# A long convolution that feeds an eight-expert layer: the third group's first input transforms moved into the first sort, its later loads asked for earlier, the filter spectrum loaded once and copied

## The chip, the core and the metric

One Trainium2 chip, one NeuronCore of it. TensorE (PE) multiplies; VectorE (DVE), ScalarE (ACT) and GpSimd (POOL) do the element-wise work, POOL also issues the gathers and scatters by row; SyncE (SP) does nothing but issue transfers, in the order in which they were written. The metric is the time of one execution in device microseconds (us).

## What is computed

Eight sequences of 5696 tokens with 128 features each are convolved along time with one filter per feature (through FFTs of twice the length), and every token of the result goes through one of eight experts, the one with the highest gate logit:

```python
L = 2 * S
Xf = np.fft.rfft(x, n=L, axis=1)
Hf = np.fft.rfft(h, n=L, axis=0)
y = np.fft.irfft(Xf * Hf[None], n=L, axis=1)[:, :S, :]
x = y.reshape(B * S, D)
logits = x @ w_gate
expert_idx = np.argmax(logits, axis=1)
for e in range(E):
    mask = expert_idx == e
    out[mask] = gate_w[mask, None] * (np.maximum(x[mask] @ w1[e], 0.0) @ w2[e])
```

## The kernel before

The batch is cut into three **groups** of 2, 3 and 3 sequences (SPLIT). Each goes through three phases, and the experts run beside the later ones.

- **Phase A** (`steps_a`, `phase_a`): the first FFT step. A loaded piece `xt` of `x` is split by ACT and DVE (or POOL) into two parts, `xc`; PE makes `pa` from it (three matmuls for the real and three for the imaginary half); a copy puts it into `ut`, and SP stores `ut` to the DRAM tensor `U`. A group of 3 has 36 such pieces: 12 rounds (`ig`) of 3 sequences. Group 0 does this alone, group 1 among the first sort, group 2 as a "guest" of the second sort (class `Guest`).
- **Phase B** (`phase_b`): the 48-point step, 120 frequencies `q`, four to a unit (`qb`). Per unit SP loads `uq` from `U`, the matrices `mt` and `mi`, and the filter's spectrum `hh` from `HS`, twice, into the upper and the lower half of the partitions. Per frequency (a **bin**): PE makes `xp` from `uq` and `mt`; DVE multiplies by the spectrum (three instructions, `zt`, `xs`, `xs`: the product); DVE or POOL adds (`combine`; DVE for the first ALONE bins); PE makes `vp` from `zt` and `mi`; ACT copies it to `vt`, which SP stores to `V`. The four steps follow each other at 1, 2, 4 and 5 bins' distance. In group 2 three of four matrices come in split form, `mt<-mqs`, and that load is issued on POOL's queue (line 456), from the third unit on.
- **Phase C**, the sort (`phase_c`): the last FFT step `yp`, its transpose `tp`, gate logits and counts `gb`, a chain of small DVE instructions that gives every token a row, and one scatter of 120 rows by POOL for each slot (`SR<-rt,pi`, line 665), with a POOL `memset` behind each but the last unit's (line 896, size REST). That memset's value is not used. It writes into a tile that the sort doesn't need: `mibufs[3]` in group 0's sort, `hhbufs[2]` in the later ones. A sort of 3 sequences has 24 units of 2 steps and 144 scatters.
- **Tables** (`tables`): some 25 small DVE instructions make from the counts the table `tab`, which says for each tile of 256 rows where its rows start and which expert it has.
- **Experts** (`experts`): per tile SP loads the rows `xr` and, where the expert changes, the weights `wb<-WD`; PE transposes (`mx`), multiplies by both layers (`mh`, `ma`), ACT and DVE take the relu (`hs`).

Every engine works through its instructions in the order in which the program wrote them; `run` writes them, by stream (experts, and `rest`, which holds the other phases), in the order of costs that are summed by hand. `rest` lets a group's tables advance by two pieces with every bin of the next phase B, and lets the experts have a group's tiles (`begin`) when the bins' summed cost is over HEAD.

All xp, vp, pa, and part of the sort's banks share four PSUM banks (tag "cx"); `mh` has two of its own.

Of the kernel before, what the change touches and what calls it, by code (L numbers as in the profile page):

```python
# [23 lines left out]
NB = 48  # L24
# [3 lines left out]
HP = 64  # L28
# [23 lines left out]
ALONE = (0, 14, 10)  # L52
HEAD = (0, 5500, 9000)
# [13 lines left out]
TABLED = 4  # L67
RATE = (0.372, 0.55, 0.28, 0.8, 1.05, 0.6)
# [3 lines left out]
def conv_moe(ctx: ExitStack, tc: tile.TileContext, I, out, B, S, D, E, F, split):  # L72
# [86 lines left out]
    state = {"rests": False, "space": False, "spare": None, "pe": 0.0, "sent": 0.0, "tail": 0}  # L159

# [13 lines left out]
    fcs = load_const("fcs", [MP, 2, QN])  # L174
# [16 lines left out]
    gcs = load_const("gcs", [QN, 2, MP])  # L191
# [7 lines left out]
    jrow = load_const("jrow", [1, total])  # L199
# [66 lines left out]
    def steps_a(gr, tag, bufs):  # L266
        g, nb = gr.g, gr.nb
        srcs = [(I["x"][gr.b0 + b], b) for b in range(nb)]
        tw = 4 * D
        items = []  # L270
        for ig in range(NB // 4):
            for src, b in srcs:
                items.append((ig, src, b))
# [4 lines left out]
        def cut(n):  # L278
            if not split or n >= len(items):
                return  # L280
# [6 lines left out]
        def load(n):  # L287
            if n >= len(items):
                return
            ig, src, b = items[n]  # L290
# [18 lines left out]
        def store(m):  # L309
            n, c = divmod(m, 2)  # L310
            ig, src, b = items[n]
            if b == 0:
                uts[c] = sb.tile([QN, 4, gr.cols], F32, tag=tag, name=f"ut{g}_{ig}_{c}", bufs=bufs)
# [11 lines left out]
        def begin(m):  # L325
            if m == 0:
                cut(0)
            if m % 2 == 0:
                load(m // 2 + fore)
                cut(m // 2 + 1)  # L330
            transform(m)

        return start, begin, store, flush, 2 * len(items)

    def phase_a(gr):
        start, begin, store, flush, M = steps_a(gr, "six", SIX - gr.g)
        half = AT if gr.g == 0 else 750 * RATE[3 * gr.g - 3]
        start()
        for m in range(M + 2):
# [4 lines left out]
            yield half  # L344
# [6 lines left out]
    class Guest:  # L351
        def __init__(self, gr):
            self.start, self.step, self.store, self.flush, self.M = steps_a(gr, "mt", MT)
# [87 lines left out]
    def phase_b(gr):  # L441
# [26 lines left out]
        def load(qb):  # L468
# [8 lines left out]
            if g != 0:  # L477
                hhs[qb] = hhbufs[qb % 3]
                for k in range(2):
# [5 lines left out]
        state, banks, late = {}, {}, []  # L485

# [81 lines left out]
        def inverse(n):  # L568
# [4 lines left out]
            vp = ps.tile([P, 512], F32, tag="cx", name=f"vp{g}_{q}_{c}", bufs=4)  # L573
# [141 lines left out]
    def phase_c(pt, guest=None):  # L715
# [156 lines left out]
        def rank(n):  # L872
# [576 lines left out]
```

## Time and profile before

| | |
|---|---|
| median of 3 runs | 2156.97 us (2149.7 to 2160.83) |
| the profiled execution | 2157.51 us, span 2155.7 us |
| PE busy | 2082.7 us, 97% of the span |
| DVE / ACT / POOL busy | 72% / 52% / 63% |
| DMA engines | share .85 to 1.0 in the first third, .5 to .8 in the second, about .35 in the last |
| granted clock of TensorE | 0.976 on average |

The span falls into stretches that can be told by the tiles in the timeline: phase A of group 0 to 100 us, phase B to 227, the first sort with phase A of group 1 to 391, phase B of group 1 with the experts from 425 on to 690, the second sort with the guest to 932, phase B of group 2 to 1345, the third sort to 1600, experts alone to the end. PE is busy in nearly all of it. It stands still or runs at the lower of its two clock levels (1.2 instead of 2.4 GHz) mainly where one stretch hands over to the next: about 380 to 430, 900 to 985 and 1605 to 1625 us. A row of the timeline has the start, the duration, the engine, the line, what is written and read, how many instructions were merged, and in brackets how long the engine had been idle before and what ended that. A row of the windows view has for each engine the busy time (and instructions) in a stretch, then the granted clock, the share of the DMA engines and GB/s.

### The profile page before, as it was taken

How to read it: one execution, taken by the hardware profiler on the slowest of the kernel's cores; microseconds unless marked ns; L12 is line 12 of the kernel's file. 1: busy time of each engine (PE TensorE's matmuls, PEld its weight loads, DVE VectorE, ACT ScalarE, POOL GpSimd, SP SyncE). 2: the span in 40 equal slices, each digit the busy share in tenths (PEclk: the TensorE clock that was granted, in tenths of full speed). 3: DMA queues.
4: the chain of work that ended last, by engine and by line, in shares of the span. 5: the costliest groups of instructions: out<-in, count | busy, mean ns of one | idle time of the engine just before them, and what ended most of it. 6: DMA issues, size and time to landing. Idle time of an engine off the chain costs nothing.

```text
span 2155.7 us, 47101 instructions
## 1 busy us (share of the span) xinstructions
PE 2082.7 (97%) x14452; PEld 1863.3 (86%) x14452; DVE 1542.5 (72%) x3373; ACT 1114.9 (52%) x2317; POOL 1350.0 (63%) x1569
## 2 busy tenths in 40 slices
PE   9999999799999999989999999999999999999998
PEld 7799777377777889878888888999999999999998
DVE  4698677799997777688888887666665555555554
ACT  5677555143334666534555555555544454444544
POOL 6566388545554388888998775288883444443333
PEclk9999999599999999999999999999999999999999
DMA  8899799999997898868878885656533244343331
GB/s 269 263 289 293 227 297 281 256 237 256 248 267 196 232 276 255 245 168 229 204 205 222 216 203 153 159 132 159 141 103 98 87 132 135 129 133 126 123 121 34
DMA packets 216993, 420.33 MB, mean 195 GB/s; under 512 B 32501, under 2 KB 136235, under 8 KB 216740
## 3 DMA queue, kind: packets, MB, share of 16 engines
q1 hardware_dynamic: 187263, 360.52, 59.7%
q0 software_dynamic: 27072, 55.35, 8.9%
q8 instruction: 117, 1.92, 0.4%
q10 hardware_dynamic: 2405, 1.43, 0.2%
q14 instruction: 136, 1.11, 0.2%
HBM read 582.45 MB, written 154.27 MB: 342 GB/s over the span
## 4 chain that ended last, share of the span: by engine, by line
PE 82%; DMA 9%; DVE 3%; POOL 2%; issue 2%; ACT 1%; SPq 1%; ACTq 0%; POOLq 0%; DVEq 0%
PE mh L167 23%; PE ma L167 22%; PE vp L167 9%; PE xp L167 9%; PE yp L167 5%; PE mx L189 4%; PE pa L167 3%; DMA xt<-x 3%; PE gb L167 2%; DMA wb<-WD 2%; DMA mt<-mq 2%; PE tp L189 1%; PE hp L167 1%; PE lb L189 1%; DMA U<-ut 1%
## 5 line engine op out<-in xcount | busy, mean ns | idle before, releaser
L1173 DVE SCALAR_TENSOR_TENSOR hs<-mh,hs 128x512 fp32r<-128x512 f32 x728 | 501.6, 689 | 387.5 <-ACT hs L1171 381.2
L167 PE MATMUL mh<-xtb,wb 128*128 128x256 f32 x4368 | 706.4, 297 | 23.0 <-DVE hs L1173 5.2
L1171 ACT ACTIVATE hs<-mh 128x512 fp32r<-128x512 f32 x728 | 435.4, 598 | 488.1 <-PE mh L167 475.4
L167 PEld LDWEIGHTS mh<-xtb,wb 128*128 128x128 f32 x4368 | 589.8, 191 | 92.6 <-issue 37.9
L167 PE MATMUL ma<-hs,wb 128*128 128x256 f32 x4368 | 658.3, 287 | 1.7 <-DMA wb<-WD 1.7
L167 PEld LDWEIGHTS ma<-hs,wb 128*128 128x128 f32 x4368 | 574.4, 191 | 2.9 <-DMA wb<-WD 2.7
L665 POOL DMA_INDIRECT SR<-rt,pi x384 | 406.0, 1057 | 196.2 <-issue 58.9
L683 POOL DMA_INDIRECT out<-xr x310 | 305.4, 985 | 354.2 <-ACT hs L1171 172.6
L566 POOL TENSOR_TENSOR zt<-zt,xs 128x384 f32<-128x384 f32 (+1 forms) x276 | 295.8, 1074 | 155.2 <-DVE xs L556 103.9
L603 ACT COPY vt<-vp 96x384 f32<-96x384 f32 x240 | 114.2, 476 | 260.8 <-PE vp L167 256.6
L560 DVE TENSOR_TENSOR xs<-xp,hh 64x384 f32<-64x384 f32 (+1 forms) x360 | 214.8, 597 | 7.8
L167 PE MATMUL vp<-zt,mi 128*96 128x384 f32 x480 | 200.5, 500 | 0.0
L551 DVE TENSOR_TENSOR zt<-xp,hh 128x384 f32<-128x384 f32 (+1 forms) x300 | 173.6, 579 | 28.7 <-PE xp L167 18.4
L167 PE MATMUL xp<-uq,mt 96*128 96x384 f32 (+1 forms) x496 | 177.7, 462 | 8.5 <-DMA uq<-U 5.1
L167 PE MATMUL pa<-xc,fcr 120*120 120x512 f32 x576 | 159.4, 411 | 1.9 <-POOL xc L284 1.0
L556 DVE SCALAR_TENSOR_TENSOR xs<-xp,hh 64x384 f32<-64x384 f32 x240 | 134.3, 560 | 4.2
L167 PE MATMUL yp<-vr,gcr 120*120 120x384 f32 x576 | 119.5, 343 | 7.1 <-ACT ut L317 7.1
L167 PEld LDWEIGHTS vp<-zt,mi 128*96 128x96 f32 x480 | 79.7, 167 | 49.8 <-issue 26.7
L167 PEld LDWEIGHTS pa<-xc,fcr 120*120 120x120 f32 x576 | 99.9, 186 | 25.2 <-DVE rk L884 2.6
L167 PEld LDWEIGHTS xp<-uq,mt 96*128 96x128 f32 x496 | 87.6, 200 | 33.5 <-issue 12.8
L317 DVE COPY ut<-pa 120x512 f32<-120x512 f32 x96 | 65.7, 684 | 68.6 <-PE pa L167 54.7
L749 DVE TENSOR_TENSOR vr<-vq,vr 120x768 fp32r<-120x768 f32 x96 | 91.5, 954 | 31.8 <-ACT vr L748 31.0
(165 smaller groups left out, 2720.9 us busy)
## 6 DMA issues: line engine op xcount, KB each, us to landing
wb<-WD SPq DMA_DIRECT2D x728, 512.0 KB
U<-ut SPq DMA_DIRECT2D x48, 720.0 KB
uq<-U SPq DMA_DIRECT2D x60, 576.0 KB
V<-vt SPq DMA_DIRECT2D x60, 576.0 KB
vq<-V SPq DMA_DIRECT2D x48, 720.0 KB
xt<-x SPq DMA_DIRECT2D x96, 240.0 KB
hh<-HS SPq DMA_DIRECT2D x120, 192.0 KB
xr<-SR SPq DMA_DIRECT2D x155, 130.0 KB
```

The lines of the kernel that those rows point to most:

```text
L167: nc.tensor.matmul(to, lhs, rhs, **kw)
L189: nc.tensor.transpose(dst, src, ident[:n, :n])
L551: nc.vector.tensor_tensor(out=zt, in0=x3, in1=hv[:, 0].broadcast_to([P, PK, cb, D]), op=ALU.mult)
L556: nc.vector.scalar_tensor_tensor(out=xs[to, 0], in0=x3[at, 0], scalar=-1.0, in1=him[:, 0], op0=ALU.mult, op1=ALU.mult)
L560: nc.vector.tensor_tensor(out=xs[to], in0=x3[at], in1=him, op=ALU.mult)
L566: eng.tensor_tensor(out=zt, in0=zt, in1=xs, op=ALU.add)
L603: done = nc.scalar.copy(outs_[qb][:, k0 : k0 + PK, c * cw : (c + 1) * cw], banks.pop(n)[:K2, :iw].rearrange("p (q x) -> p q x", q=PK),)
L665: s = nc.gpsimd.indirect_dma_start(out=SR[:, :], out_offset=IndirectOffsetOnAxis(ap=pi[:, b : b + 1], axis=0), in_=rt[:, b, :], in_offset= ...
L683: sc = nc.gpsimd.indirect_dma_start(out=out[:, :], out_offset=IndirectOffsetOnAxis(ap=xr[:, s, D + 1 : D + 2].bitcast(I32), axis=0), in_=x ...
L749: nc.vector.tensor_tensor(out=vr[:, 1], in0=src, in1=vr[:, 0].bitcast(F32), op=ALU.subtract)
L1171: done = nc.scalar.activation(hs[:, 0], hp, AF.Relu)
L1173: done = nc.vector.scalar_tensor_tensor(out=hs[:, 1], in0=hp, scalar=0.0, in1=hs[:, 0].bitcast(F32), op0=ALU.max, op1=ALU.subtract)
```

## The change

Seven edits:

1. `phase_a` of group 1 goes on with the first round of group 2: three pieces, six transforms, their six copies all on ACT, two stores to `U`. The guest of the second sort starts from the second round.
2. `phase_b` of group 2 is entered when the second sort writes its last unit's second step, and then asks for the first two units' inputs; its bins follow after the sort, as before.
3. From the third unit on `hh` is loaded once, and ACT copies it to the other partitions in two halves.
4. POOL's filler memset writes into the FFT constants that are no longer needed (`spent`).
5. ALONE of group 1 from 14 to 5: `combine` of bins 5 to 13 from DVE to POOL. HEAD of group 1 from 5500 to 7000: the experts may start two bins later.
6. `vp` of group 1 takes its PSUM bank from `mh`'s two as long as no expert has started.
7. `tables` has one expert per partition, sums over experts by small matmuls (`ah`, `rj`), and has 13 pieces where it had 11.

```diff
-ALONE = (0, 14, 10)
-HEAD = (0, 5500, 9000)
+ALONE = (0, 5, 10)
+HEAD = (0, 7000, 9000)
+AFORE = 1
+SLOW = 2.0
...
+    spent = const.tile([MP, 4, QN], F32, name="spent")
+    fcs, gcs = spent[:, :2], spent[:, 2:]
...
+        items = work(gr)[AFORE * nb :] if after else work(gr)
+        if g == 1:
+            items += work(groups[2])[: AFORE * groups[2].nb]
+        own = len(work(gr))
...
-            cp = nc.scalar.copy if c == 0 else nc.vector.tensor_copy
+            cp = nc.scalar.copy if c == 0 or n >= own else nc.vector.tensor_copy
             cp(uts[c][:, :, b * D : (b + 1) * D], srcv)
             if b == nb - 1:
-                late.append((gr.U[:, lo : lo + 4, :], uts[c]))
+                late.append((to.U[:, lo : lo + 4, :], uts[c]))
...
-            yield half
+            yield half * (SLOW if m >= own else 1)
...
-                for k in range(2):
+                for k in range(2 if qb < 2 else 1):
                     nc.sync.dma_start(hhs[qb][k * HP : k * HP + NB, :QB], HS[:, q : q + QB])
...
+        def double(qb, at):
+            if g and 2 <= qb < QN // QB:
+                hh = hhs[qb][:, at : at + QB // 2]
+                nc.scalar.copy(hh[HP : HP + NB], hh[:NB])
...
-            vp = ps.tile([P, 512], F32, tag="cx", name=f"vp{g}_{q}_{c}", bufs=4)
+            tag, bufs = ("mh", 2) if g == 1 and not live else ("cx", 4)
+            vp = ps.tile([P, 512], F32, tag=tag, name=f"vp{g}_{q}_{c}", bufs=bufs)
...
+        if ask:
+            yield 0
...
+                if k0 == 0:
+                    double(qb, QB // 2)
+                if k0 == QB - 1:
+                    double(qb + 1, 0)
...
-                    idle = hhbufs[2].rearrange("p a b d -> p (a b d)") if g else mibufs[3].rearrange("p a x -> p (a x)")
-                    nc.gpsimd.memset(idle[:, : REST[g]], 0.0)
+                    nc.gpsimd.memset(spent.rearrange("p c q -> p (c q)")[:, : REST[g]], 0.0)
...
+                if guest and (n, k) == (nu - 1, 1):
+                    assert guest.m == guest.M
+                    guest.bins = phase_b(guest.gr, True)
+                    next(guest.bins)
...
-        for k in range(E):
-            if k % 4 == 0:
-                yield
-            e = E - 1 - k if down else k
-            a, b = (e + 1, e) if down else (e, e + 1)
-            nc.vector.tensor_tensor(out=end[:, b : b + 1], in0=end[:, a : a + 1], in1=nt[:, e : e + 1], op=ALU.add)
...
+        bank = ps.tile([P, 512], F32, tag="cx", name=f"ah{g}", bufs=4)
+        mm(bank[:E1, 0:1], tcol[:, 7 + E1 * down : 7 + E1 + E1 * down], nt, start=True, stop=True)
...
+        nc.vector.tensor_scalar(out=begun, in0=jr, scalar1=ahead, scalar2=here, op0=ALU.is_ge, op1=ALU.mult)
...
+        mm(bank[:1, :NT], tcol[:, 5:6], begun, start=True, stop=False)
...
-            bins = phase_b(gr)
+            bins = guest.bins if guest else phase_b(gr)
```

What this does to the order, at the three places that matter here. SP, where the first sort ends and phase B of group 1 begins (`U_72` and `U_74` are the `U` of group 1 and of group 2). Before:

```order
L298 DMA U_72<-ut_11_0_4379 120x1536
L298 DMA U_72<-ut_11_1_4426 120x1536
L259 DMA WD<-wsp_4146 128x1024
L264 DMA WD<-wsp_4294 128x1024
L459 DMA mt_0_4709<-mq 96x512
L473 DMA uq_0_4711<-U_72 96x4x384
```

Now:

```order
L307 DMA U_72<-ut_11_0_4382 120x1536
L265 DMA WD<-wsp_4147 128x1024
L307 DMA U_72<-ut_11_1_4431 120x1536
L270 DMA WD<-wsp_4295 128x1024
L307 DMA U_74<-ut_0_0_4616 120x1536
L307 DMA U_74<-ut_0_1_4623 120x1536
L471 DMA mt_0_4759<-mq 96x512
L485 DMA uq_0_4761<-U_72 96x4x384
```

Two stores of group 2 have come between the last stores of the first sort and the first loads of phase B. PE at the same place, the end of the first sort (`gb` are logits and counts, `xp_0` is the first bin). Before:

```order
L167 MATMUL gb_15_None<-c_moe_w_gate,yt_15_4594 120x8 x6
L167 LDWEIGHTS ones
L167 MATMUL gb_None_4674<-oh_15_4668,ones 128x54
L167 LDWEIGHTS lt
L167 MATMUL gb_None_4674<-oh_15_4668,lt 120x54
L167 MATMUL xp_0_0_4725<-uq_0_4711,mt_0_4709 128x384
```

Now:

```order
L170 MATMUL gb_15_None<-c_moe_w_gate,yt_15_4630 120x8 x6
L170 MATMUL pa_38_0_4696<-xc_38_4518,fcr 120x512 x3
L170 LDWEIGHTS ones
L170 MATMUL gb_None_4715<-oh_15_4709,ones 128x54
L170 LDWEIGHTS lt
L170 MATMUL gb_None_4715<-oh_15_4709,lt 120x54
L170 MATMUL pa_38_1_4746<-xc_38_4518,fcr 120x512 x3
L170 MATMUL xp_0_0_4775<-uq_0_4761,mt_0_4759 128x384
```

The last two of the six added transforms stand around the sort's last counts, the very last one directly ahead of the first bin. POOL at the end of the second sort, where phase B of group 2 begins (`rt_22` and `rt_23` are the rows of the sort's last two units, `mt_8` and `mt_12` hold the split matrices of bins 8 to 11 and 12 to 15). Before:

```order
L665 DMA SR<-rt_22_12329,pi_22_12605 366848x130
L896 MEMSET hh_111 128x288
L665 DMA SR<-rt_23_12482,pi_23_12711 366848x130 x6
L683 DMA out<-xr_7692 45568x128
L456 DMA mt_8_12791<-mqs 96x768
L683 DMA out<-xr_7887 45568x128 x2
L683 DMA out<-xr_8084 45568x128 x2
L456 DMA mt_12_12996<-mqs 96x768
```

Now:

```order
L689 DMA SR<-rt_22_12330,pi_22_12633 366848x130
L919 MEMSET spent 120x288
L689 DMA SR<-rt_23_12463,pi_23_12735 366848x130 x6
L707 DMA out<-xr_7792 45568x128
L468 DMA mt_8_12787<-mqs 96x768
L707 DMA out<-xr_7792 45568x128
L707 DMA out<-xr_7990 45568x128 x2
L707 DMA out<-xr_8191 45568x128
L468 DMA mt_12_12997<-mqs 96x768
```

The filler writes into another tile, but nothing has moved on POOL: `mt_8` stands behind all of the sort's scatters in both.

## Rows read from the trace of the kernel before

**Rows 1.** The page, busy time of PE, its share of the span, instructions.
```profile
PE 2082.7 (97%) x14452; PEld 1863.3 (86%) x14452; DVE 1542.5 (72%) x3373; ACT 1114.9 (52%) x2317; POOL 1350.0 (63%) x1569
```

**Rows 2.** Windows: stretch, busy us (instructions) of each engine, granted clock, DMA share, GB/s.
```profile
400.00:420.00 20.00, 16.95 (x24) 6.03 (x24) 19.05 (x47) 2.37 (x5) 8.82 (x10) 0.50 0.95 263
...
500.00:520.00 20.00, 20.00 (x115) 15.14 (x114) 18.70 (x35) 8.62 (x19) 10.96 (x11) 1.00 0.95 241
```

**Rows 3.** Timeline, PE, first hand-over: start, us, instruction, idle before it.
```profile
394.07 5.46 PE L167 MATMUL xp<-uq,mt 96*128 96x384 f32 x8 [2.72 <-DMA uq<-U]
...
403.83 1.65 PE L167 MATMUL xp<-uq,mt 96*128 96x384 f32 x2 [0.56 <-ACT vt L603]
...
425.12 1.89 PE L167 MATMUL mh<-xtb,wb 128*128 128x256 f32 x6 [0.46 <-ACT xtb L1155]
...
430.64 0.96 PE L167 MATMUL vp<-zt,mi 128*96 128x384 f32 x2
```

**Rows 4.** Timeline, SP, the same hand-over.
```profile
385.26 1.23 SPq L473 DMA_DIRECT2D uq<-U  x1
...
388.28 0.89 SPq L480 DMA_DIRECT2D hh<-HS  x2
...
413.21 1.99 SPq L1134 DMA_DIRECT2D wb<-WD  x4
416.64 2.61 SPq L1106 DMA_DIRECT2D xr<-SR  x3
```

**Rows 5.** Timeline, DVE, from the first product to the table.
```profile
396.15 0.56 DVE L551 TENSOR_TENSOR zt<-xp,hh 128x384 f32<-128x384 f32 x1 [2.35 <-DMA hh<-HS]
...
412.27 0.18 DVE L1042 TENSOR_TENSOR tab<-ej 1x36 int32<-1x36 f32 x1
```

**Rows 6.** Timeline, PE, second sort's end and phase B of group 2.
```profile
905.64 2.28 PE L167 MATMUL yp<-vr,gcr 120*120 120x384 f32 x6 [3.15 <-ACT ut L317]
...
917.98 1.62 PE L167 MATMUL pa<-xc,fcr 120*120 120x512 f32 x6
...
934.87 0.88 PE L167 MATMUL xp<-uq,mt 96*128 96x384 f32 x2 [1.66 <-DMA uq<-U]
...
955.70 0.95 PE L167 MATMUL mh<-xtb,wb 128*128 128x256 f32 x6 [3.32 <-DVE r L1020]
...
968.60 0.70 PE L167 MATMUL xp<-us,mt 96*128 96x384 f32 x3
...
978.04 1.62 PE L167 MATMUL mh<-xtb,wb 128*128 128x256 f32 x6 [3.64 <-DVE xs L556]
...
984.11 0.87 PE L167 MATMUL ma<-hs,wb 128*128 128x256 f32 x6
```

**Rows 7.** Timeline, SP, around the blocked load of `hh`.
```profile
953.90 0.78 SPq L480 DMA_DIRECT2D hh<-HS  x2
...
955.49 0.53 SPq L1134 DMA_DIRECT2D wb<-WD  x2
```

**Rows 8.** Timeline, POOL, first and last scatter of the second sort, and after.
```profile
730.50 1.33 POOL L665 DMA_INDIRECT SR<-rt,pi  x1 [40.28 <-ACT hs L1171]
...
960.58 1.00 POOL L665 DMA_INDIRECT SR<-rt,pi  x1 [0.30 <-DMA SR<-rt,pi]
...
962.87 0.60 POOL L456 DMA_DIRECT2D mt<-mqs  x1
...
966.37 0.97 POOL L683 DMA_INDIRECT out<-xr  x1 [0.30 <-DMA mt<-mqs]
```

**Rows 9.** Timeline, SP, one unit's loads in phase B of group 1.
```profile
505.10 0.32 SPq L473 DMA_DIRECT2D uq<-U  x1
...
507.99 0.83 SPq L480 DMA_DIRECT2D hh<-HS  x2
...
516.55 0.33 SPq L473 DMA_DIRECT2D uq<-U  x1
```

**Rows 10.** Lines by form, ACT, nearest to the added copies: busy us, mean ns, idle.
```profile
L538 ACT CAST us<-uq 96x384 fp32r<-96x384 f32 x84 | 42.7, 508 | 0.0
```

More of the change, by code (lines that the diff above doesn't have):

```diff
@@ L352, in __init__ @@
         def __init__(self, gr):
-            self.start, self.step, self.store, self.flush, self.M = steps_a(gr, "mt", MT)
+            self.start, self.step, self.store, self.flush, self.M, _ = steps_a(gr, "mt", MT, True)
             self.gr, self.m, self.open = gr, 0, []
@@ L987, in tables @@
-        start = sb.tile([1, E + 1], F32, tag="start", name=f"start{g}")
-        nc.vector.memset(start, float(E * CAP))
-        here, after = (start[:, high], start[:, low]) if down else (start[:, low], start[:, high])
-        if prior is not None:
-            nc.vector.tensor_tensor(out=here, in0=prior, in1=ahead, op=ALU.subtract)
-        else:
-            nc.vector.tensor_scalar(out=here, in0=ahead, scalar1=-1.0, scalar2=None, op0=ALU.mult)
-        nc.vector.scalar_tensor_tensor(
-            out=here, in0=here, scalar=float(T), in1=base0[0:1, :E], op0=ALU.mult, op1=ALU.add
-        )
@@ new lines, in tables @@
+        nc.vector.tensor_scalar(out=ended, in0=jr, scalar1=upto, scalar2=here, op0=ALU.is_ge, op1=ALU.mult)
+        nc.vector.tensor_scalar(out=over, in0=jr, scalar1=upto, scalar2=None, op0=ALU.is_ge)
+        yield
+        yield
+        yield
+        bank = ps.tile([P, 512], F32, tag="cx", name=f"rj{g}", bufs=4)
+        mm(bank[:1, :NT], tcol[:, 5:6], begun, start=True, stop=False)
+        mm(bank[:1, :NT], tcol[:, 6:7], ended, start=False, stop=True)
+        mm(bank[:1, 128 : 128 + NT], tcol[:, 5:6], over, start=True, stop=True)
@@ L1015, in tables @@
+        mm(bank[:1, 256:257], nt, tcol[:, 1:2], start=True, stop=True)
         yield
         r0 = sb.tile([1, NT], F32, tag="r0", name=f"r0{g}", bufs=1)
-        nc.vector.tensor_reduce(out=r0, in_=ge.rearrange("p e j -> p j e"), axis=AX.X, op=ALU.add)
+        ej = sb.tile([1, NT], F32, tag="ej", name=f"ej{g}", bufs=1)
+        nc.vector.scalar_tensor_tensor(
+            out=r0, in0=jr[0:1], scalar=float(T), in1=bank[:1, :NT], op0=ALU.mult, op1=ALU.add
+        )
+        nc.vector.tensor_scalar(
+            out=ej, in0=bank[:1, 128 : 128 + NT], scalar1=float(E - 1), scalar2=None, op0=ALU.min
+        )
@@ L1018, in tables @@
+        pt.need = const.tile([1, 1], I32, name=f"need{g}")
+        nc.vector.tensor_copy(pt.need, bank[:1, 256:257])
         yield
-        nc.vector.scalar_tensor_tensor(out=r0, in0=jr, scalar=float(T), in1=r0, op0=ALU.mult, op1=ALU.add)
-        nc.vector.tensor_scalar(out=r0, in0=r0, scalar1=start[:, none : none + 1], scalar2=None, op0=ALU.add)
         tab = const.tile([1, 3, NT], I32, name=f"tab{g}")
         nc.vector.tensor_scalar(out=tab[:, 0, :], in0=r0, scalar1=float(E * CAP), scalar2=None, op0=ALU.min)
-        yield
@@ L1042, in tables @@
         nc.vector.tensor_tensor(out=tab[:, 2, back:], in0=ej[:, back:], in1=ej[:, : NT - back], op=ALU.not_equal)
+        pt.tab = tab
         yield
-        pt.need = const.tile([1, 1], I32, name=f"need{g}")
-        nc.vector.tensor_copy(pt.need, end[:, E - none : E - none + 1])
-        pt.tab = tab
         if not last:
@@ L1049, in tables @@
             nc.vector.tensor_copy(state["left"], ej[:, NT - 1 :])
-        if not last:
-            did = sb.tile([1, E], F32, tag="did", name=f"did{g}")
+            did = sb.tile([E1, 1], F32, tag="did", name=f"did{g}")
             nc.vector.tensor_scalar(
```

102 lines of the change are left out of this document (56 added, 46 removed).

## The prediction

> **What bounds the kernel now.** I read the page's engine line first: PE is busy 2082.7 of 2155.7 us, 97%, and no other engine comes near [rows 1]. The windows say where the rest is. In the body of phase B PE is busy for 20.00 of 20 us at full clock although the DMA engines are at .95 [rows 2], so there neither fewer bytes nor a shorter ACT or DVE chain can shorten anything. In 400 to 420, where the first sort hands over to phase B of group 1, PE is at 16.95 of 20 with a granted clock of 0.50, the lower level (1.2 GHz), and DVE at 19.05. Then I read the timeline at the hand-overs, for the brackets: who ended each stop of PE, and what that one had waited for. Only such stops, and the matmuls at the lower clock behind them, can be won. The profiled execution (2157.51 us) lies 0.5 us from the median, so I sum on 2157.5.
>
> **First hand-over: six transforms, two stores, combines on POOL, HEAD.** Before, the sort's last matmul ended 2.72 us ahead of `xp_0` at 394.07, which waited for `uq_0`, asked for at 385.26: 8.8 us from issue to use [rows 3, 4]. The six added transforms are 18 matmuls; six take 1.62 us, about 1.46 from start to start, so 4.4 us in all [rows 6], and they fall among the sort's own waits for DVE: I let the sort end 0.6 us later. They are free on PE. What they issue is not. By the order, SP now has two stores of group 2 ahead of `mt_0` and `uq_0`, and the second can leave only when ACT has copied the very last transform, which PE makes directly ahead of `xp_0`. So `uq_0` is asked for not at 385.3 but at about 393.8: sort's end at 392, half a us for the copy (0.51 is the nearest row [rows 10]), one issue of 1.2 us as `uq`'s own [rows 4]. That is 8.5 us later, and with the same landing the first product moves from 396.15 to about 404.5. Queued behind it are `mi`, `hh`, the next units' loads; the waiter is PE, and DVE with the product.
>
> From the first product to the table it was 16.1 us on DVE (412.27 less 396.15 [rows 5]), which runs products, five combines and some 25 small instructions in one queue. The new `tables` has about 20 instructions and five combines stay (ALONE 5); the two extra pieces of a half bin each are paid by shorter instructions. I keep 16.1: `tab` at 420.6. The weights followed it 0.9 us later and the rows 4.4 us later [rows 4]; `mx` came without a wait about 1 us ahead of the first `mh` (425.12 [rows 3]), so the rows landed within 7.4 us. By that the first `mx` is at 425 to 432.4; the transfers ahead of it being as dense as before, I take 431. By then PE has its 13 bins (HEAD): 30 us for as many steps before (394.07 to the first `mx`), less 8 times 0.56, the wait for a bank at each bin [rows 3], which the banks of `mh` take away, from 402.6: about 428. So `mh` stands at about 432 with 13 bins done. Before, PE had done 13 bins and as much of the experts at about 430.5 [rows 3]. **Cost: +1.5 us.** Bounds: -3 when the rows land as early as PE is through with the bins; +6 when they need the whole 7.4 us and `uq_0` is held longer. The nine combines go to POOL at no cost: it was busy for 8.82 of 20 us there [rows 2].
>
> At this place rows 2 and 3 show a PE that stops 0.56 us in every bin and stays at the lower clock until 430.64, where a pair of `vp` takes 0.96 instead of 1.49 us. The Trainium skill, "TensorE: Matmul & The Clock Gate", section "A second HAM failure mode: psum-queue depth-cycling", says that a PE that idles briefly between groups because it cycles through PSUM banks makes the clock gate oscillate, and that the price is the slow matmuls between the bursts. That would put the clock back some bins earlier once `vp` has its own banks; the sum would be about 2 us lower. It bears on a time that the table sets, so I leave it in the range.
>
> **Second hand-over: earlier loads, filler elsewhere, fewer transforms.** Here three things really go. `hh` of the third unit was issued only at 953.90, 19 us after the first bin's matmul at 934.87: its tile was the target of the filler memset behind the scatters. SP stood, and the weights queued behind it left at 955.49 [rows 7]; PE's stop of 3.32 us ahead of `mh` at 955.70 is that [rows 6]. With the filler in `spent` SP goes through. The first loads are asked for a sort step earlier, so the 1.66 us that PE waited for `uq` goes. And 4.4 us of transforms are gone from the guest, with perhaps the 3.15 us at 905.64.
>
> But the next thing is POOL. The scatters run without a gap from 730.50 to 961.6, 144 of them with their fillers [rows 8]; the change takes none away, and the filler is of the same length. Behind the last scatter stands `mt_8<-mqs`, issued at 962.87 and landed by 966.1, when POOL goes on [rows 8]. `xp_8` at 968.60 needs it [rows 6]. So however early PE comes (by the terms above some 12 us earlier), it can't make `xp_8` before about 966.1: 2.5 us are won and the rest is a new stop, ended by that DMA. **Gain: 2.5 us**, bounds 0 and 5 (scatters starting a little earlier or later).
>
> **Behind it.** At 978.04 PE stopped 3.64 us for DVE's product, and ran at the lower clock from there to 984.11, where `ma` takes 0.87 again: 6.1 us of which half, about 2.9 us, is lost (six `mh` 1.62 against 0.95 [rows 6]). If DVE has used the new stop to come level, both go: -6.5. The new stop, of some 10 us, has a price of the same kind, about 2.5. **Net -4**, bounds -6.5 and +2.5.
>
> **The copies and the rest.** Per unit ACT gets two copies of 48 x 512. The nearest row is 0.51 us at 384 columns [rows 10]; by columns 0.68, so 112 copies are 57 to 76 us, on an ACT that has 8.62 of 20 us in use [rows 2], beside PE. Instead 56 loads of 192 KB go, from DMA engines that don't bound PE there. Taken at 0; what hides them is ACT's idle time, and the rival below is what they cost without it. The third group's tables and the handful of small matmuls: within 0.5 us, taken at 0.
>
> **Sum:** 1.5 - 2.5 - 4 = -5; 2157.5 - 5 = 2152.5, rounded to **2152**. Bounds of all terms together, with little chance that all go one way: 2143 to 2164.
>
> **Rivals.**
> - *The second hand-over's stops go altogether*: `xp_8` doesn't wait for `mt_8`, because POOL starts its scatters enough earlier, or later work covers the stop. Then 4.4 + 3.15 + 1.66 + 3.32 + 3.64 + 2.9 = 19.1 us are won, less 1.5: **2140**. For it: each is a bracket in rows 6. Against it: POOL's row of scatters without a gap. Chance .18.
> - *ACT's copy comes too early (slower)*. The copy of a unit's first half stands in ACT's queue at the end of the unit ahead and waits for `hh`. `hh` is asked for four bins ahead; a unit took 11.45 us, and SP needs 3.7 us from `uq` until `hh` is issued [rows 9], which leaves 7.7. The one landing that the rows show, from 388.28 to 396.15, is 7.9 from the start of the issue, 7.0 from its end [rows 4, 5]. So the margin is about nothing. If the copy waits, relu and `vt` wait behind it in order, and PE for these. It decides as soon as the landing takes over 7.7 us; at 0.5 us a unit, 56 units make 28 us: **2180**. Against it: half the bytes, and a backlog on ACT of half a us is caught up by an engine that idles half the time. Chance .14.
> - *The stores hold phase B for longer* (+6 to +9 at the first hand-over, the gains behind as forecast): **2158**. Chance .12.
> - That the change doesn't do what it says: the order shows each edit in its place but one. The earlier loads of group 2 can't bring `mt_8`; that is in the forecast.
>
> **How the numbers follow.** Forecast .56, of which about a sixth below 2146. Half a per cent, 10.8 us, is about what a measurement of this kernel can tell from no change: faster is below 2146.2, slower above 2167.8. Faster: .18 + .09 = .27; slower: .14 less what of it stays within, .13; same: .60. The range of 8 in 10 leaves out a third of the first rival, most of the second and a little of the forecast: 2138 to 2168.
>
> **What would show it.** First hand-over: `xp_0` near 402.5, its wait ended by `uq<-U`, the second `U` store on SP ahead of it; first `mh` near 432; no 0.56 us waits for `vt`. If `xp_0` comes at 394, the store doesn't hold, and the term turns to -3. Second hand-over: no SP gap ahead of `hh`, no wait of 1.66; a PE stop of 8 to 12 us ahead of the ninth `xp` ended by DMA `mt<-mqs`, and scatters ending within 2 us of 961.6. If that stop is missing, the first rival holds. ACT's copies with brackets <-DMA `hh<-HS` in every unit, and PE below 20.00 in the windows of phase B, would be the second rival. The forecast is wrong as a whole when time moves in the stretches where PE is busy throughout.

## The result, and the profile after

The changed kernel is slower: 2170.71 us in the median of 7 runs (2163.13 to 2182.09) against 2156.97, also of 7; the ratio is 1.0069, interval 1.0043 to 1.0096. Run a second time it gave 1.0068 (1.0046 to 1.0090). The forecast was 2152, its range ended at 2168. The profiled execution is the slowest of its runs (2182.09 us, span 2180.2); 10 us of its distance arose in phase B of group 0, whose code is as it was, and in the second profile of the same kernel only 3. So times below are taken between marks within one trace, and sizes of whole edits from ratios.

The page's engine line, then windows of the two hand-overs and of phase B's body (stretch, busy time of PE, PEld, DVE, ACT, POOL, granted clock, DMA share, GB/s):

```profile
PE 2078.1 (95%) x14482; PEld 1864.9 (86%) x14482; DVE 1524.8 (70%) x3333; ACT 1186.7 (54%) x2432; POOL 1357.0 (62%) x1578
```

```profile
400.00:420.00 20.00, 5.51 (x11) 2.39 (x11) 4.38 (x17) 1.50 (x3) 16.50 (x23) 0.53 0.93 235
420.00:440.00 20.00, 15.07 (x43) 6.66 (x44) 19.10 (x50) 5.78 (x11) 3.28 (x3) 0.84 0.98 222
480.00:500.00 20.00, 20.00 (x114) 15.15 (x113) 18.61 (x35) 11.00 (x24) 10.62 (x11) 1.00 0.88 219
980.00:1000.00 20.00, 8.63 (x44) 7.31 (x45) 6.26 (x12) 4.32 (x9) 15.74 (x18) 0.66 0.50 139
```

PE's work is nearly the same, 2078 us instead of 2083, but the span is 24.5 us longer: the time went into stops. In the body PE is still busy for 20.00 of 20, with ACT at 11.00 (480 to 500) where it had 8.62 (500 to 520) [rows 2]. In 400 to 420 it works 5.51 us. The timeline of PE says why, at the first hand-over, at the end of phase B of group 1, and at the second hand-over (start, duration, instruction, in brackets the idle time before and what ended it):

```profile
400.64 1.23 PE L170 MATMUL pa<-xc,fcr 120*120 120x512 f32 x3
415.23 4.18 PE L170 MATMUL xp<-uq,mt 96*128 96x384 f32 x6 [13.36 <-DMA uq<-U]
...
424.92 0.85 PE L170 MATMUL xp<-uq,mt 96*128 96x384 f32 x2
...
436.78 0.91 PE L170 MATMUL xp<-uq,mt 96*128 96x384 f32 x2 [1.41 <-DVE xs L573]
...
438.64 1.50 PE L170 MATMUL xp<-uq,mt 96*128 96x384 f32 x2
...
445.67 0.69 PE L194 MATMUL mxNone<-ident,xr 128*128 128x128 f32 x2 [2.58 <-DMA xr<-SR]
...
453.68 0.81 PE L170 MATMUL xp<-uq,mt 96*128 96x384 f32 x2
...
715.76 1.62 PE L170 MATMUL mh<-xtb,wb 128*128 128x256 f32 x6 [6.28 <-DMA wb<-WD]
...
991.37 1.33 PE L170 MATMUL xp<-us,mt 96*128 96x384 f32 x3 [13.76 <-DMA mt<-mqs]
```

The queue of SP at the first and at the second of these places (end of phase B), POOL at the third, from its first scatter on, and DVE's first product and table at the first:

```profile
400.94 1.90 SPq L307 DMA_DIRECT2D U<-ut  x2
402.93 1.61 SPq L471 DMA_DIRECT2D mt<-mq  x1
404.64 1.09 SPq L485 DMA_DIRECT2D uq<-U  x1
...
703.06 0.33 SPq L667 DMA_DIRECT2D V<-vt  x1
707.75 1.06 SPq L754 DMA_DIRECT2D vq<-V  x1
709.53 1.08 SPq L1161 DMA_DIRECT2D wb<-WD  x2
```

```profile
756.50 1.32 POOL L689 DMA_INDIRECT SR<-rt,pi  x1 [53.92 <-ACT xc L292]
...
985.68 1.00 POOL L689 DMA_INDIRECT SR<-rt,pi  x1 [0.30 <-DMA SR<-rt,pi]
...
987.97 0.61 POOL L468 DMA_DIRECT2D mt<-mqs  x1
```

```profile
418.35 0.56 DVE L568 TENSOR_TENSOR zt<-xp,hh 128x384 f32<-128x384 f32 x1 [15.22 <-DMA hh<-HS]
...
434.17 0.18 DVE L1068 TENSOR_TENSOR tab<-ej 1x36 int32<-1x36 f32 x1
```

Against the rows of before: `xp_0` waited 2.72 us for `uq_0` [rows 3] and now waits 13.36; `uq_0` leaves at 404.64, behind the two stores, the second of which could go only after the last transform of 400.64. The wait of 0.56 us per bin for a bank is gone. From 424.92 a bin's `xp` take 0.85 instead of 1.65, at the higher clock level instead of the lower, but PE now waits for DVE's products (1.41 us at 436.78), and from 438.64 to 453 its matmuls are long again (1.50), at a granted clock of 0.67 from 440 to 450. At 707.75 stands a wait that was not spoken of: the first sort load `vq` has gone ahead of the experts' weights. And the ninth `xp` waits for `mt<-mqs` behind the scatters, as forecast; their train lasts 230 us as before [rows 8], only 26 us later.

Four marks on ACT cut each trace into stretches: the sort's copies to `rt` (32 in the first sort, 48 in each other), phase B's copies to `vt` (120 in each of two groups) and the experts' relu `hs`. In us:

| from, to | before | changed | again |
|---|---|---|---|
| last `rt` of first sort to first `hs` | 47.1 | 58.2 | 57.0 |
| the same to the 21st `vt` | 75.8 | 82.6 | 80.8 |
| last `vt` of group 1 to second sort's first `rt` | 20.7 | 28.7 | 27.9 |
| first to last `rt` of the second sort | 215.3 | 206.7 | 205.8 |
| last `rt` of the second sort to the 21st `vt` of group 2 | 104.3 | 111.2 | 107.5 |
| from that 21st `vt` to the last | 313.4 | 311.4 | 310.4 |
| last `rt` of the third sort to the last `hs` | 556.9 | 563.2 | 563.4 |

### The profile page after: what moved, and what is told of

Read it like the earlier page. It is cut to its first block, busy times and chain, and to the rows that moved or that the text cites. A ratio compares the mean times of both kernels' runs of the same rounds, so it can differ in the third digit from the quotient of the medians.

```text
span 2180.2 us, 47181 instructions
## 1 busy us (share of the span) xinstructions
PE 2078.1 (95%) x14482; PEld 1864.9 (86%) x14482; DVE 1524.8 (70%) x3333; ACT 1186.7 (54%) x2432; POOL 1357.0 (62%) x1578
## 4 chain that ended last, share of the span: by engine, by line
PE 81%; DMA 7%; POOL 4%; DVE 3%; issue 2%; SPq 1%; ACT 1%; POOLq 0%; ACTq 0%; DVEq 0%
PE mh L170 22%; PE ma L170 22%; PE vp L170 8%; PE xp L170 8%; PE yp L170 5%; PE pa L170 4%; PE mx L194 3%; PE gb L170 2%; DMA wb<-WD 2%; POOL SR L689 2%; PE tp L194 1%; DMA mt<-mq 1%; DMA xt<-x 1%; PE lb L194 1%; PE hp L170 1%
## 5 line engine op out<-in xcount | busy, mean ns | idle before, releaser
L583 POOL TENSOR_TENSOR zt<-zt,xs 128x384 f32<-128x384 f32 (+1 forms) x285 | 305.0, 1072 | 161.8 <-DVE xs L573 105.1
L919 POOL MEMSET spent<- 120x288 f32 (+1 forms) x366 | 127.3, 348 | 0.5
```

The lines of the kernel that those rows point to most:

```text
L583: eng.tensor_tensor(out=zt, in0=zt, in1=xs, op=ALU.add)
L919: nc.gpsimd.memset(spent.rearrange("p c q -> p (c q)")[:, : REST[g]], 0.0)
```

## The experiments

Ratios are to the kernel before on the same chip, with their 95% intervals; 0.001 is 2.2 us. The changed kernel is 1.0069 and 1.0068, measured in other runs than e1 to e4, so a difference of two ratios has an interval of some 6 to 8 us to either side.

**e1: the two stores on ACT's queue.**

```diff
-                nc.sync.dma_start(*late.pop(0))
+                to, fr, eng = late.pop(0)
+                eng.dma_start(to, fr)
...
-                late.append((to.U[:, lo : lo + 4, :], uts[c]))
+                late.append((to.U[:, lo : lo + 4, :], uts[c], nc.scalar if n >= own and not after else nc.sync))
```

> The changed kernel with one edit: the two added stores to the third group's U leave from ACT's DMA queue, right behind ACT's last copy, no longer from SP's. Nothing else moves. Theory (the stores hold phase B): in the changed kernel PE stood 13.36 us ahead of the first bin, ended by uq_0, which SP asked for at 404.64 behind those stores; now SP asks about 8 to 10 us earlier and PE's stop falls to 3 to 5 us, and the time falls by 5 to 9 us against the changed kernel (2170.7 to about 2164). Rival (the landing is what is slow: the stores' 1.44 MB are in flight beside the loads either way, or the loads wait for the tiles that the stores read): SP asks earlier, but the stop stays over 9 us and the time within 3 us of 2170.7.

Measured 1.0026 (1.0002 to 1.0050), 9 us off the changed kernel's ratio. The PE and SP rows of this kernel, and who held that `mt` on SP in e8 below, which has the same stores on ACT (us, times, longest):

```profile
396.30 4.18 PE L170 MATMUL xp<-uq,mt 96*128 96x384 f32 x6 [3.97 <-DMA uq<-U]
...
408.67 1.62 PE L170 MATMUL xp<-uq,mt 96*128 96x384 f32 x2 [6.03 <-DVE zt L584]
```

```profile
388.72 0.32 SPq L486 DMA_DIRECT2D uq<-U  x1
...
390.13 0.93 SPq L493 DMA_DIRECT2D hh<-HS  x2
400.43 0.32 SPq L472 DMA_DIRECT2D mt<-mq  x1
```

```profile
SPq L472 <- DMA U<-ut: 9.4, 1, 9.4
```

`uq_0` leaves before the last transform, and PE stops 3.97 us instead of 13.36; the first relu comes 52.1 us after the sort, no longer 57 to 58. So the stores' place on SP holds `uq_0`. But they aren't out of the way: the second unit's `mt` leaves SP 9 us after `hh`. In e8 SP waits there for the landing of the first store, which signals by the same semaphore (101) as this `mt`; the second store and the `uq` behind it share another (102). So PE stops a second time, 6.03 us ahead of the fifth bin (6.87 in e8, 6.80 in e10, ended by `uq<-U` there; at most 0.73 in e3, e11 and e15, which have no such stores). The rival's slow landing is borne out here, one unit later.

**e2: `mt_8` asked for ahead of the last scatters.**

```diff
         if ask:
+            load_m(2)
             yield 0
...
-                if k0 == 1:
+                if k0 == 1 and not (ask and qb == 0):
```

> The changed kernel with one edit: the split matrices of the third unit of group 2 (mt_8) are asked for together with the first two units' inputs, so that on POOL they stand ahead of the last two and a half units' scatters instead of behind all. Theory (POOL's train of scatters sets when the ninth bin can start): the stop of 13.76 us ahead of the first xp from us goes to under 2 us, and the time falls by 8 to 14 us (2170.7 to 2157 to 2163), unless the next stop behind it takes part of it back. Rival (PE only trades stops: the scatters still end where they do, and the experts' first tiles or DVE's products are late next): stops of the same sum appear within the next 40 us and the time falls by less than 4 us.

Measured 1.0069 (1.0049 to 1.0090): nothing gained. PE, SP and POOL of this kernel at the second hand-over:

```profile
966.33 0.69 PE L170 MATMUL xp<-us,mt 96*128 96x384 f32 x3
...
991.40 1.62 PE L170 MATMUL mh<-xtb,wb 128*128 128x256 f32 x6 [15.40 <-DMA wb<-WD]
```

```profile
980.44 0.36 SPq L1134 DMA_DIRECT2D xr<-SR  x1
...
983.82 0.79 SPq L1162 DMA_DIRECT2D wb<-WD  x2
```

```profile
975.47 1.00 POOL L690 DMA_INDIRECT SR<-rt,pi  x1 [0.30 <-issue]
```

```profile
SPq L1134 <- DMA out<-xr: 17.8, 1, 17.8
```

The ninth `xp` (966.33) no longer waits, and four bins on PE stops 15.40 us. The experts' next rows `xr` leave at 980.44, and the weights stand behind them on SP. What held `xr` for 17.8 us was, by the last line, the experts' own write `out<-xr`, which POOL issues behind the last scatter of 975.47. What stands behind the scatters is late, whichever transfer it shows itself by; the rival held.

**e3: edits 1 and 2 undone.**

```diff
-AFORE = 1
+AFORE = 0
...
-                    guest.bins = phase_b(guest.gr, True)
-                    next(guest.bins)
...
-            bins = guest.bins if guest else phase_b(gr)
+            bins = phase_b(gr)
```

> The changed kernel without its edits 1 and 2: all 36 pieces of the third group are the guest's again, and phase B of group 2 asks for its first inputs only when the second sort is through; edits 3 to 7 (one load of hh and copies, filler elsewhere, ALONE, HEAD, vp's banks, tables) stay. Theory (the loss at the first hand-over is the stores', the new stop at the second is the earlier arrival): the first bin's stop falls from 13.36 to about 3 us, the time to 2158 to 2164, and at the second hand-over PE comes later and stops less than 6 us ahead of the ninth xp. Rival (the loss is in edits 3 to 7, ACT's copies above all): the time stays at 2168 or above.

Measured 1.0002 (0.9984 to 1.0021). First relu 47.6 us after the sort as before (47.1); `xp_0` waits 4.50 us; ahead of the ninth `xp` 6.12 us. The second sort takes 213.1 us again. So 14 us, nearly all of the loss, go with edits 1 and 2, and the rival that puts it into edits 3 to 7 is out. HEAD is still 7000 here and its stretch still long (27.0 us, see e4), so the other edits must give about as much back.

**e4: HEAD of group 1.**

```diff
-HEAD = (0, 7000, 9000)
+HEAD = (0, 5500, 9000)
```

> The changed kernel with HEAD of group 1 back at 5500, so that the experts may start two bins earlier, which also puts the experts half a tile to one tile further at each later place. Theory A (the 15 us lost between the first hand-over and the second sort's start come in part from the order of SP's loads: at the end of phase B vq stood ahead of the weights, and PE stopped 6.28 us for wb there where it had stopped 2.08): the time from the last vt copy to the sort's first rt copy falls from 28.7 towards the 20.7 us of before, the time by 3 to 8 us. Theory B (that stretch differs from run to run, and HEAD costs nothing): within 3 us of the changed kernel.

Measured 1.0041 (1.0023 to 1.0060), 6 us off the changed kernel, at the edge of what the intervals tell apart; the stretch tells more. From phase B's last `vt` to the sort 22.5 us instead of 28.7. In all kernels with 7000 this stretch took 26.8 to 28.9 us, in all with 5500 19.3 to 22.5. PE and SP here, and for the changed kernel what SP waited for ahead of `vq` (698 to 712; us, times, longest):

```profile
703.80 0.93 PE L170 MATMUL mh<-xtb,wb 128*128 128x256 f32 x6 [1.50 <-DMA wb<-WD]
```

```profile
698.75 1.42 SPq L1161 DMA_DIRECT2D wb<-WD  x2
701.14 0.48 SPq L1133 DMA_DIRECT2D xr<-SR  x1
702.30 1.05 SPq L754 DMA_DIRECT2D vq<-V  x1
```

```profile
SPq L754 <- DMA V<-vt: 4.3, 1, 4.3
```

The weights leave here ahead of `vq`, which has to wait for the last `V` store, and PE stops 1.50 us instead of 6.28.

**e5: the changed kernel again.** No edit.

> The changed kernel itself, as the one to hold the next three against on the same chip, and a second profile of it. Theory (its loss has fixed places: the first hand-over, the end of phase B of group 1, the tail's tables): the ratio to before is again 1.005 to 1.009; the first expert's relu comes 8 to 12 us later than in the kernel before, counted from the last matmuls of the first phase B; and the 11 us that the first profile lost in phase B of group 0, whose code did not change, are gone. Rival (that loss belongs to the change): they are there again.

1.0068 (1.0046 to 1.0090). The table above has its stretches: the same places, and the loss in group 0 went from 10 to 3 us.

**e6: `hh` loaded twice** (edit 3 undone).

```diff
-                for k in range(2 if qb < 2 else 1):
+                for k in range(2):
...
-            if g and 2 <= qb < QN // QB:
+            if False:
```

> The changed kernel with edit 3 undone: hh is loaded twice from memory for every unit, and ACT copies nothing. Theory A (in the bodies of phase B, from the 20th to the last vt copy, the changed kernel is 2 us faster in group 1 and 4 to 5 us faster in group 2, and the copies instead of loads are why): that gain goes, the time rises by 4 to 7 us against the changed kernel. Theory B (the gain comes from somewhere else, as the table's shape or the filler): the bodies stay as they are, and the time stays within 3 us. The second rival of the prediction (ACT's copy holds relu and vt) would make it faster by 20 us.

1.0110 (1.0090 to 1.0131), 9 us above the changed kernel. The stretch from the 21st to the last `vt` of group 2 took 316.5 us, not 310.4. PE's waits there (1020 to 1340), in this kernel and in the changed one run again:

```profile
PE ma L170 <- DMA wb<-WD: 5.3, 3, 3.2
PE mh L170 <- DMA wb<-WD: 0.5, 1, 0.5
```

```profile
PE mh L170 <- DMA wb<-WD: 1.2, 1, 1.2
PE ma L170 <- DMA wb<-WD: 0.8, 1, 0.8
```

The waits for the experts' weights, which stand on SP's queue with the second load, sum to 5.8 us instead of 2.0; that is 3.8 of the 6.1 us.

**e7: the old tables** (edit 7 undone: `tables` of the kernel before, word for word but for its row of numbers).

```diff
...
-        jr = jrow[:, :NT]
+        jr = jrow[0:1, :NT]
...
```

> The changed kernel with edit 7 undone: the function that makes the tables is that of the kernel before. Theory (the new tables have two pieces more, the third group's pieces stand one by one among the last expert tiles, and table and first rows come later for it): at the end, from the first of the table's instructions to the table, 29.6 to 31.5 us go back to about 24, the time from the last rt copy to the end falls by 5 us, and the time by 4 to 7 us; at the first hand-over the table comes 1 to 3 us sooner too. Rival (those 5 us are a slower stretch of weights and clock, not the table): the end stays as long, the time within 3 us.

1.0069 (1.0052 to 1.0085): the tables cost or give nothing. The end stays at 562.0 us; my guess that they lengthen it is wrong.

**e8: the three places together** (the diffs of e1, e4 and e7).

> The changed kernel with three edits that the places above point to: the two added stores leave from ACT's queue, HEAD of group 1 is 5500 again, and the tables are those of the kernel before. What stays of the change: the transforms in the first sort, the earlier loads, the copies of hh, the filler's place, ALONE and vp's banks. Theory (the loss is the sum of these three places): 5 to 7 us from the stores, 3 to 5 from HEAD, 4 to 6 from the tables, so 12 to 17 us faster than the changed kernel and a ratio to the kernel before of 0.998 to 1.002. Rival (the scatters on POOL set when the third group may start, so what is won ahead of the second sort is won, what is won within it is not, and the rest of the loss sits in a place not yet seen): a ratio above 1.003.

0.9993 (0.9975 to 1.0011). From 1.0068 that is 16 us, about what e1 (9), e4 (6) and e7 (0) sum to. Sort to first relu is 48.8 us, end of phase B to the second sort 20.7, and the end 552.8.

**e9: e8 with a shorter filler in the second sort.**

```diff
-REST = (224, 288, 288)
+REST = (224, 128, 288)
```

> The combined kernel (stores on ACT's queue, HEAD 5500, old tables) with the filler memset of the second sort cut from 288 to 128 columns. By the rows of the two sizes (361 ns at 288, 309 at 224 columns) that is 0.13 us for each of 138 fillers, 18 us off the train of scatters. Theory (the end of that train, 230 us behind its first scatter whatever PE does, sets when the ninth xp of group 2 and the next rows of the experts may start): the last scatter comes 14 to 18 us sooner after the first, PE's stop of 5.78 us ahead of the ninth xp falls under 1 us, and the time falls by 5 to 10 us against the combined kernel (ratio to before 0.994 to 0.997). Rival (the fillers keep the scatters from standing in each other's way, so that each takes longer without them): the scatters' mean goes from 1055 to over 1150 ns, the train's end moves less than 5 us, and the time within 3 us of the combined kernel, or above it.

1.0130 (1.0105 to 1.0156), the rival's side but not by its mechanism: a scatter takes 1060 ns as ever, and from the first start to the last the train is 246 instead of 229 us long. The waits of POOL from 720 to 985 and of ACT from 740 to 960 (us in all, times, longest):

```profile
POOL SR L690 <- ACT hs L1200: 29.1, 11, 5.0
```

```profile
ACT ut L327 <- remote: 21.0, 4, 6.5
```

POOL now catches up with ACT and waits for it, and the sort itself is slower, 239.0 us from first to last `rt` instead of 206.7. ACT stood four times, 21.0 us, ahead of a copy into `ut`, ended by an event that the trace ties to no instruction; a `U` store stood ahead of each such tile. That the denser scatters delay those stores would fit; it isn't shown.

**e10: e8 with edit 2 undone** (inputs of group 2 asked for after the sort).

```diff
-                if guest and (n, k) == (nu - 1, 1):
-                    assert guest.m == guest.M
-                    guest.bins = phase_b(guest.gr, True)
-                    next(guest.bins)
...
-            bins = guest.bins if guest else phase_b(gr)
+            bins = phase_b(gr)
```

> The combined kernel with edit 2 undone: phase B of group 2 is entered, and its first loads asked for, only when the second sort is through. Theory (the end of the scatters sets the ninth xp, so an earlier ask buys a longer stop there and nothing else): a stop for uq of 1.5 to 3.5 us comes back ahead of the first xp, the stop ahead of the ninth is shorter by as much, and the time stays within 3 us. Rival (the early loads are worth their 1.66 us and the bins ahead of the ninth can be used): 3 to 6 us slower.

0.9977 (0.9961 to 0.9993). No stop for `uq` of the size expected came back, and no loss; with 0.9993 for e8 the earlier ask buys nothing that can be told. The second sort takes 212.6 us and the hand-over behind it 104.2, together 316.8; with the ask (e8) 206.7 and 108.5, together 315.2.

**e11: the changed kernel without edits 1 and 2, HEAD 5500, old tables** (the diffs of e3, e4 and e7).

> The changed kernel without its edits 1 and 2, with HEAD 5500 and the old tables: what is left of the change is one load of hh with ACT's copies, the filler's place, ALONE and vp's banks. Theory (edit 1 costs 1 to 6 us at the first hand-over even with the stores on ACT, because the loads behind still come later, and its 4.4 us in the second sort are not seen behind the scatters): 2 to 6 us faster than the combined kernel, ratio to before 0.996 to 0.998. Rival (with its stores out of the way edit 1 pays, by the shorter second sort): 3 us or more slower than the combined kernel.

0.9971 (0.9948 to 0.9993); again, as e15, 0.9983 (0.9968 to 0.9999). It lies with e10 on the same chip, which differs from it by edit 1 with the stores on ACT: a cost or a gain of edit 1 in that form can't be told, within some 6 us. It is 5 us faster than e8, as the theory had it, but the rival of 3 us is excluded only narrowly.

**e12 and e13: e11 with edit 4, or with ALONE and `vp`'s banks, undone as well.**

```diff
-                    nc.gpsimd.memset(spent.rearrange("p c q -> p (c q)")[:, : REST[g]], 0.0)
+                    idle = hhbufs[2].rearrange("p a b d -> p (a b d)") if g else mibufs[3].rearrange("p a x -> p (a x)")
+                    nc.gpsimd.memset(idle[:, : REST[g]], 0.0)
...
-ALONE = (0, 5, 10)
+ALONE = (0, 14, 10)
...
-            tag, bufs = ("mh", 2) if g == 1 and not live else ("cx", 4)
+            tag, bufs = ("cx", 4)
```

> The kernel of the eleventh run (changed kernel without edits 1 and 2, HEAD 5500, old tables) with edit 4 undone as well: the filler memset writes into the hh tile again, as before. The prediction put 3.32 us of PE's stop on SP's wait there and let only 2.5 us of the hand-over be won. Theory (the end of the scatters sets that hand-over, so the freed SP buys a stop further on): SP's load of hh is held again until the last filler, PE's stops move from the ninth xp to the bins ahead of it, and the time rises by less than 3 us against the eleventh run (ratio to before 0.996 to 0.999). Rival (the freed queue is worth its 3.3 us and the weights behind): 4 to 7 us slower, ratio 0.999 to 1.001.

> The kernel of the eleventh run with edits 5 (its ALONE part) and 6 undone as well: DVE adds for 14 bins again, and vp shares the four banks. Theory (the first rows of the experts are what the first hand-over waits for: the eleventh run's PE stops 3.00 us for xr, so the bins' own pace is hidden): PE stops 0.56 us in every bin again and runs at the lower clock there, but the first relu comes within 2 us of where it was, counted from the sort's last rt copy, and the time stays within 2 us. Rival (clock and banks are what the first hand-over is worth): 4 to 6 us slower.

1.0011 (0.9991 to 1.0031) and 1.0000 (0.9983 to 1.0018), on another chip than e11. Both lie 0.2 to 0.4 per cent above it, at the edge of the intervals, and the traces don't show where. With the filler back the third unit's `hh` leaves SP 12.8 us after the first bin instead of 8.7 (e11) and 9.0 (e15), but PE's stops from that bin to the ninth sum to 10.1 us as they do without (9.9 and 10.3), with none ahead of the ninth in all three: the freed queue is not seen at PE. Also with the filler back the second sort and the hand-over take 327.0 us (e11 322.3, e15 318.5); with ALONE and the banks back the first relu comes 48.8 us after the sort (47.4, 46.1), and PE waits for a bank again:

```profile
410.09 1.65 PE L170 MATMUL xp<-uq,mt 96*128 96x384 f32 x2 [0.56 <-ACT vt L621]
```

By their ratios both stay inconclusive.

**e14, e15, e16: the copies on the kernel before (edit 3's lines added to it), e11 again, e11 without the copies (e6's diff).**

> The kernel before with edit 3 alone: hh is loaded once from the third unit on and ACT copies it. Theory (the copies are worth what undoing them cost, 0.4 per cent, since they take 10.7 MB from the DMA queues): 6 to 10 us faster than the kernel before, ratio 0.995 to 0.997. Rival (in the kernel before, where the experts stand half a tile further, those loads are hidden, and the 0.4 per cent belongs to the changed order alone): within 3 us, ratio 0.9986 to 1.0014. The prediction's value was 0.

> The kernel of the eleventh run again (changed kernel without edits 1 and 2, HEAD 5500, old tables), as the one to hold the next against on one chip. What is left of the change in it is the copies of hh, the filler's place, ALONE and vp's banks. If the edits add up, the ratio is that of the copies alone or up to 0.002 below it; if the filler, ALONE and the banks cost something, it is above it by over 0.002.

> The kernel of the eleventh run with edit 3 undone too, hh loaded twice. Theory: 6 to 10 us slower than the eleventh, by as much as in the changed kernel. Rival: within 3 us of it, so that the copies are worth something only where the rest of the change has put the loads.

0.9987 (0.9968 to 1.0005), 0.9983 (0.9968 to 0.9999), 1.0008 (0.9986 to 1.0029), on one chip. The copies are worth 3 us alone (within the interval of nothing), 5 in the reduced change, 9 in the changed kernel. Only the gain in the changed kernel is clear of its interval, and the three sizes are not told apart. The stretch from the 21st to the last `vt` of group 2, where e6 shows the gain, doesn't show it in the other two pairs: 314.4 us with the copies (e14) and 313.4 without (before), 314.5 with (e15) and 312.2 without (e16).

## Why the prediction was wrong, by its steps

**The first hand-over: right mechanism, its cost of +1.5 us mis-sized.** The step said that the second store holds `uq_0`, that it would be asked for 1.8 us after the sort's end, and that the net cost is +1.5 us, at most +6. In the trace it is asked for 2.8 us after the last transform's end (400.64 + 1.23 to 404.64: the copy, the store, and `mt`, whose issue of 1.6 us the step left out), and it needs 10.6 us to its use where it had needed 8.8 [rows 3, 4]. From there the chain ran nearly as forecast: the table 15.8 us behind the first product (16.1), `mx` 11.5 us behind the table (10.4). So the first `mh`, with 13 bins done, came 53.3 us after the sort's last `rt`; the time that the step set against it, 430.5 before, is 47.6. That is +5.7 us. Then the clock fell again (below): the 21st `vt` came 5 to 7 us later with two relu fewer done. By e1's ratio the place of the stores is worth 9 us. That is the third rival's mechanism, at the lower end of its size (+6 to +9) by the trace and at the upper by the ratio. The sort itself was let end 0.6 us later; in the ten profiles with edit 1 it takes 150.3 us from first to last `rt` on average, in the eight without 148.0.

**HEAD: the step that failed outright.** I priced it as two bins' shift at its own place, at nothing. It shifts the experts against everything behind: one relu fewer by the end of phase B, and in that order SP has `vq`, which waits for the last `V` store, ahead of the weights. The stretch grew by 6 to 8 us in every kernel with 7000, and e4's ratio gives 6. The order of SP at the end of phase B would have shown it; the step went only by the places that the diff names.

**The second hand-over: right mechanism, gain at its size or under it.** Forecast: a stop of 8 to 12 us ahead of the ninth `xp`, ended by `mt<-mqs`, the train of scatters unchanged, -6.5 us with what lies behind it. Measured: 13.76 and 11.68 us of stop by that DMA, a train of 230 us, and from the second sort's first `rt` to the 21st `vt` of group 2 -1.7 and -6.3 us. e2 shows that the end of the scatters is the bound: with the wait that shows it removed the next transfer behind them stops PE as long; that the early loads change nothing (e10) fits. So the first rival, all stops gone (2140), could not come. One reading under it was wrong: PE's stop of 3.32 us at 955.70 was put down to SP's wait for the filler, but its row names DVE (`r`), the weights left only 0.21 us before it ended [rows 6, 7], and e12 finds PE's stops there the same with the filler back.

**The copies: taken at 0, worth something.** ACT's copy takes 618 ns, inside the bounds given, and the second rival (2180) is refuted by its waits in the changed kernel: of 112 copies three waited for `hh`, 4.9 us in all.

```profile
L502 ACT COPY hh<-hh 48x512 f32<-48x512 f32 x112 | 69.2, 618 | 7.6 <-DMA hh<-HS 4.9
```

A gain of up to 9 us was missed because I read a PE at 20.00 of 20 in a window as proof that the DMA never bounds there; e6 shows short waits for weights that such a window doesn't contain. This holds for the changed kernel; in the other two orders the gain lies within or at the edge of its interval.

**The clock and the banks.** The Trainium skill ("TensorE: Matmul & The Clock Gate", "A second HAM failure mode: psum-queue depth-cycling") describes a clock that oscillates where PE idles briefly between groups because it cycles through PSUM banks. The prediction took from it that the clock would be back some bins earlier with `vp` in its own banks. In the changed kernel the `xp` are short again at 424.92, ten microseconds after the first bin, but after stops of 0.69 to 1.41 us, mostly for DVE, they are long from 438.64 on, and short for good only at 453.68: 38 us after the first bin, as before (38; 37 by the `vp` of [rows 3]). In the kernels with the banks and without edit 1 it is 26 (e12), 30 (e16), 33 (e15), 37 (e11) and 38 (e3), without the banks 36 (e14) and 39 (e13). So the traces bear this out in part at most: the clock can be back earlier with the banks, but behind the bank PE waited for DVE. Of the 4.5 us that the step took off for the banks (8 times 0.56) about half came: PE was through its 13 bins 27.9 us after the first began, not 25.5.

**What stays open.** The last stretch, from the third sort to the end, is 5 to 10 us longer with HEAD 7000 (562.0 to 566.8) than the 556.9 of before, and in e8 to e16 it is not (552.8 to 559.2); one relu more to do is 1.6 us of it. In e4 (HEAD 5500, new tables) it was 562.0 too, in e7 (7000, old tables) 562.0, and neither edit is shown to be the cause. Nor is it settled what e12 and e13 differ by. The bounds of the prediction's terms (+6, 0, +2.5) add up to 2166 at the top, not to 2164; the range to 2168 holds either, and the result lies above it.

The best version is e11 (and e10): 0.2 to 0.3 per cent faster than the kernel before. Of the edits, the copies point to a gain by ratio in all three places where they were tried, clearly in one, and two lose: the stores on SP (e1, e3) and HEAD (e4 and its stretch).

## What to carry to other kernels

An instruction that is moved takes its stores along: put work into a neighbour's idle slots only after looking at which in-order queue its stores enter, and what loads stand behind them there. Another queue helps, but a load that shares a semaphore with such a store still waits for it to land. A number that shifts one stream against another has to be read at every later hand-over, not at its own. And when several waits end together, look for the one train of work that they have in common: taking away one of them moves the stop, not the end.

## What was not expected of the hardware

The filler memsets between the scatters are worth their time: cut from 288 to 128 columns, which saves 0.13 us each, they make the kernel 30 us slower (0.9993 to 1.0130), with scatters of the same 1060 ns. Why is not shown. The end of phase B of group 0, whose code did not change, lay 9.5 us later than in the kernel before in one profile of the changed kernel and 2.7 in the other, so a stretch is worth comparing only between marks close by.
